# First loads of a four-layer kernel: x blocks in order on one DMA queue, first weights on the other, one warm-up matmul fewer

## The chip, the cores and the metric

The kernel runs on one core of a Trainium2 chip. The metric is the device time of one execution in microseconds (us), given as the median of several. "Before" and "after" are the kernel without and with the change. The record marks every execution as fast, and all of them are compared. Medians of a run and of the kernel before beside it are from the same chip; traces compared with each other are from several.

## The reference, cut to what matters

```python
x = A_x                                            # (1, 2048, 1024) bf16
x = x + A(layernorm(x), A_wqkv, A_wo)              # linear attention, 32 heads
x = x + B(layernorm(x), B_W_gate, B_W_up, B_W_down)   # gated MLP, F = 3584
x = x + A(layernorm(x), A_wqkv, A_wo)
x = x + B(layernorm(x), B_W_gate, B_W_up, B_W_down)
```

Almost all the time is matmuls of 128x128 by 128x512 (in the trace before, TensorE is busy for 1613.2 of 1625.4 us). The change touches only the start: the first blocks of x (128 rows each) are loaded, normalised and transposed, while the first weights (the k columns of `A_wqkv`, two blocks k0 and k1 of 1 MB) are loaded. The first useful matmul needs both.

## The kernel before

```python
def head(self):
    H = self.KT // 2                                   # 4 of the 8 k-tiles
    zero = self.ep.tile([P, NW], BF16, tag="e")
    nc.vector.memset(zero, 0.0)
    idle = self.ps3.tile([P, NW], F32, tag="b")
    for _ in range(11):                                # warm-up of TensorE, result unused
        nc.tensor.matmul(idle, lhsT=zero[:, 0:P], rhs=zero, start=True, stop=True)

    k0, k1, v0, q0, q1 = (ring.place() for _ in range(5))
    self.load_x(0, 0)                   # first half of x block 0, SyncE's queue
    self.load_x(0, 1, nc.scalar)        # second half, ScalarE's queue
    k0(0, H)                            # k0a: 512 KB of weights, SyncE
    self.load_x(1, None, nc.scalar)     # x block 1, 256 KB, ScalarE
    k0(H, 2 * H)                        # k0b
    self.load_x(2); k1(); self.load_x(3)
    # ... (cut)

def block0():                           # the order of the first work
    stat(0, 0); stat(0, 1); rstd(0)     # VectorE, VectorE, VectorE + ScalarE
    stat(1, 0)                          # VectorE needs x block 1 HERE ...
    scale(0, 0); scale(0, 1)            # ... before it scales block 0
    t0 = turn(0, 0); t1 = turn(0, 1)    # TensorE transposes block 0
    t0("ss"); stat(1, 1); rstd(1)
    # ... (cut)
    k(0, 0, between)                    # first useful matmuls: 4 with k0a, then 4 with k0b
```

In what follows x0, x1 and x2 are the first blocks of x. The program puts the first statistics of x1 before the scaling of x0. In the trace before, x1 landed at 5.53 us and its statistics started at 5.55; x0's statistics were ready at 5.87, and its scaling starts at 6.16, behind those of x1: an earlier x1 could gain about 0.3 us there (an estimate, 6.16 less 5.87).

Of the kernel before, what the change touches and what calls it, by code (L numbers as in the profile page):

```python
# [80 lines left out]
class _Net:  # L81
# [131 lines left out]
    def head(self):  # L213

        nc, tc, ring = self.nc, self.tc, self.ring
        H = self.KT // 2

        zero = self.ep.tile([P, NW], BF16, tag="e")
        nc.vector.memset(zero, 0.0)
        idle = self.ps3.tile([P, NW], F32, tag="b")  # L220
        for _ in range(11):
            nc.tensor.matmul(idle, lhsT=zero[:, 0:P], rhs=zero, start=True, stop=True)

        k0, k1, v0, q0, q1 = (ring.place() for _ in range(5))
        self.load_x(0, 0)
        self.load_x(0, 1, nc.scalar)
        k0(0, H)
        self.load_x(1, None, nc.scalar)
        k0(H, 2 * H)
        self.load_x(2)  # L230
        k1()
        self.load_x(3)

        def load():
            for t in range(4, 8):
                self.load_x(t)
            q1()
            for t in range(8, self.ST):
                self.later.at(3 + (t - 8) // 2 * 2, lambda t=t: self.load_x(t))
            self.later.at(11, v0)  # L240

        src = self.xb
        self.xnT[0, 0] = self.xnTp.tile([P, self.KT, QT * P], BF16, tag="xnT", name="xnT0_0")
        stats = [self.small.tile([P, 2, nc.vector.BN_STATS_DIM], F32, tag="stats", name=f"st{j}")
                 for j in range(QT)]
        rs, xn = {}, {}

        def stat(j, c):
            self.ln_stat(j, src[j], c, stats[j])

        def rstd(j):
            rs[j] = self.ln_rstd(stats[j])
            xn[j] = self.xn_home(0, j)

        def scale(j, h=None):
            self.ln_scale(src[j], *rs[j], xn[j], h)

        def turn(j, h):
            tp = self.ps3.tile([P, H, P], BF16, tag="b")
            for i in range(H):  # L260
                kt = h * H + i
                nc.tensor.transpose(tp[:, i, :], xn[j][:, kt * P:(kt + 1) * P], self.ident)  # L262
            dst = self.xnT[0, 0][:, h * H:(h + 1) * H, j * P:(j + 1) * P]

            def take(engine):
                if engine == "v":
                    nc.vector.tensor_copy(out=dst, in_=tp)
                elif engine == "s":
                    nc.scalar.activation(out=dst, in_=tp, func=ACT.Copy)
                else:  # L270
                    for i in range(0, H, 2):
                        nc.scalar.activation(out=dst[:, i:i + 2, :], in_=tp[:, i:i + 2, :],  # L272
                                             func=ACT.Copy)

            return take

        return load, q0, H, xn, stat, rstd, scale, turn
# [466 lines left out]
```

## Time and profile before

| | before |
|---|---|
| median (3 runs) | 1627.14 us (1626.99 to 1627.36) |
| profiled span | 1625.4 us |
| TensorE busy | 1613.2 us, 99% |
| x1 lands / first transposes / first useful matmul | 5.53 / 6.62 / 7.49 us |
| k0a, k0b, k1 land | 6.1, 7.6, 11.3 us |

The lines of the profile are in the prediction. In a chain of waits each piece is start, length, what; a DMA piece lasts from its issue to its landing. Lines of single groups give start, length, engine (SPq and ACTq are the sequencers of SyncE and ScalarE as they issue DMAs), source line and count. In lines of DMA queues q1 is SyncE's and q10 ScalarE's.

### The profile page before, as it was taken

Reading aid. Unit: us, or ns where it says so; the run is one execution under the profiler, and the core shown is the slowest. Engines: PE = TensorE matmul, PEld = TensorE weight load, DVE = VectorE, ACT = ScalarE, POOL = GpSimd, SP = SyncE. Lnnn points to the kernel's source line nnn. Section 1 sums busy time; section 2 is a strip of 40 time slices with the busy share of each in tenths; the row PEclk is TensorE's granted clock in tenths of the full one; section 3 lists DMA queues with packets and bytes.
Section 4 is the critical chain, followed back from the end, with each engine's and each line's share of the span. In section 5 each row is a group of like instructions: output and inputs, shape, how many; then the busy total and the mean of one; then the engine's idle time right before and its main releaser. Section 6 shows DMA issues by size and latency. Waiting matters only on the chain.

```text
span 1625.4 us, 18607 instructions
## 1 busy us (share of the span) xinstructions
PE 1613.2 (99%) x7605; PEld 739.4 (45%) x7739; DVE 567.7 (35%) x940; ACT 330.4 (20%) x635; POOL 202.1 (12%) x134
## 2 busy tenths in 40 slices
PE   9999999999999999999999999999999999999999
PEld 4444444444444444444444444444444444444444
DVE  8844694113212222222264447932021112111211
ACT  6741212101110210111067312121011101101110
POOL 1449220000000000000023582100000000000000
PEclk9999999999999999999999999999999999999999
DMA  9314547447455545544550157464654455454442
GB/s 269 55 52 66 172 79 203 146 158 215 156 162 195 156 147 165 160 154 139 166 111 1 54 107 240 86 189 145 193 161 152 154 178 155 146 170 150 155 162 71
DMA packets 300358, 235.58 MB, mean 145 GB/s; under 512 B 103408, under 2 KB 296304, under 8 KB 300272
## 3 DMA queue, kind: packets, MB, share of 16 engines
q1 hardware_dynamic: 294192, 228.75, 48.3%
q10 hardware_dynamic: 6080, 5.64, 1.0%
q8 instruction: 60, 0.98, 0.3%
q14 instruction: 26, 0.21, 0.0%
HBM read 201.33 MB, written 8.39 MB: 129 GB/s over the span
## 4 chain that ended last, share of the span: by engine, by line
PE 99%; issue 0%; DMA 0%; DVE 0%; ACT 0%
PE pu L643 24%; PE pg L643 24%; PE acc L667 23%; PE ps L410 14%; PE ps L536 7%; PE ps L445 7%; PE kv L458 0%; PE acc_last L667 0%; DMA x<-in_A_x_dram 0%; PE fold L521 0%; PE tp L262 0%; PE ps L435 0%; ACT L692 0%; DVE xo L684 0%; DVE x L156 0%
## 5 line engine op out<-in xcount | busy, mean ns | idle before, releaser
L643 PEld LDWEIGHTS <-t 128*128 128x128 bf16 x3584 | 350.7, 98 | 422.8
L643 PE MATMUL pu<-xnT,t 128*128 128x512 bf16 x1756 | 420.1, 379 | 2.0
L643 PE MATMUL pg<-xnT,t 128*128 128x512 bf16 x1756 | 419.8, 379 | 1.8
L667 PE MATMUL acc<-t,hT 128*128 128x512 bf16 x1728 | 380.6, 379 | 1.9
L649 DVE TENSOR_TENSOR hT<-pu,rg 128x512 bf16<-128x512 f32 x224 | 154.8, 691 | 571.5 <-PE pu L643 555.0
L648 ACT ACTIVATE rg<-pg 128x512 f32<-128x512 f32 x224 | 133.5, 596 | 736.1 <-PE pg L643 661.7
L667 PEld LDWEIGHTS <-hT 128*128 128x128 bf16 x1820 | 178.1, 98 | 209.0
L410 PE MATMUL ps<-t,xnT 128*128 128x512 bf16 x1024 | 223.4, 379 | 0.2 <-ACT xnT L272 0.2
L410 PEld LDWEIGHTS <-xnT 128*128 128x128 bf16 x1024 | 99.4, 98 | 120.0 <-issue 1.5
L536 PE MATMUL ps<-T,pqT 128*128 128x512 bf16 x500 | 110.2, 379 | 0.6
L147 ACT ACTIVATE rstd<-mv,eps 128x1 f32<-128x1 f32 x64 | 18.8, 294 | 337.7 <-DVE mv L145 337.5
L684 DVE TENSOR_TENSOR xo<-x,acc 128x512 bf16<-128x512 f32 x31 | 21.3, 687 | 170.3 <-PE acc L667 169.5
L489 POOL TENSOR_TENSOR prod<-pq,zrow 128x1024 f32<-128x1024 bf16 x32 | 68.0, 2125 | 85.9 <-DVE den L494 72.4
L140 DVE BATCH_NORM_STATS2 stats<-x 128x6 f32<-128x512 f32 (+1 forms) x120 | 77.9, 671 | 1.2 <-DMA x<-in_A_x_dram 0.4
L536 PEld LDWEIGHTS <-pqT 128*128 128x128 bf16 x512 | 49.9, 98 | 60.4 <-issue 0.5
L425 POOL CAST ksum<-x 128x512 f32<-128x512 bf16 x2 | 1.7, 866 | 605.4 <-DVE x L361 605.4
L681 DVE TENSOR_TENSOR x<-x,acc 128x512 f32<-128x512 f32 x32 | 21.6, 674 | 138.5 <-PE acc L667 137.4
L427 POOL TENSOR_TENSOR ksum<-ksum,slab 128x512 f32<-128x512 f32 x46 | 54.1, 1183 | 80.3 <-DVE slab L361 63.0
L361 DVE SCALAR_TENSOR_TENSOR pq<-ps,e 128x512 bf16<-128x512 f32 x64 | 43.9, 686 | 53.3 <-ACT e L355 51.3
L501 POOL TENSOR_TENSOR pq<-pq,den 128x1024 bf16<-128x1024 bf16 x32 | 61.7, 1936 | 3.1 <-DVE den L496 3.1
L494 DVE TENSOR_REDUCE den<-prod 128x32 f32<-128x1024 f32 x32 | 38.9, 1217 | 54.0 <-POOL prod L489 54.0
L445 PE MATMUL ps<-slab,x 128*128 128x512 bf16 x249 | 55.7, 379 | 0.4
(57 smaller groups left out, 592.5 us busy)
## 6 DMA issues: line engine op xcount, KB each, us to landing
t<-in_B_W_gate_dram SPq DMA_DIRECT2D x56, 1024.0 KB, 7.3
t<-in_B_W_up_dram SPq DMA_DIRECT2D x56, 1024.0 KB, 5.4
t<-in_B_W_down_dram SPq DMA_DIRECT2D x64, 896.0 KB, 5.1
t<-in_A_wqkv_dram SPq DMA_DIRECT2D x10, 1024.0 KB, 5.1
t<-in_A_wo_dram SPq DMA_DIRECT2D x4, 1024.0 KB, 6.7
away<-x SPq DMA_DIRECT2D x8, 512.0 KB, 4.7
x<-away SPq DMA_DIRECT2D x8, 512.0 KB, 8.2
out_dram<-xo ACTq DMA_DIRECT2D x31, 128.0 KB, 2.5
```

The lines of the kernel that those rows point to most:

```text
L140: self.nc.vector.bn_stats(out=stats[:, c, :], in_=src[:, c * fmax:(c + 1) * fmax])
L361: nc.vector.scalar_tensor_tensor(out=out, in0=ps, scalar=0.0, in1=e, op0=ALU.max, op1=ALU.add)
L410: nc.tensor.matmul(by_row(ps), lhsT=self.xnT[l, l_q][:, kt, j * P:(j + 1) * P], rhs=w[:, kt, :].rearrange("p (b i d) -> p i b d", i=R, d=H ...
L427: nc.gpsimd.tensor_tensor(out=ksum[:, cols], in0=ksum[:, cols], in1=pk, op=ALU.add)
L445: nc.tensor.matmul(ps, lhsT=self.xn[l, t][:, d * P:(d + 1) * P], rhs=self.pk[l, t][:, h * NW:(h + 1) * NW], start=(t == 0), stop=(t == sel ...
L489: nc.gpsimd.tensor_tensor(out=prod, in0=pq_of[sc, j], in1=zrow, op=ALU.mult)
L501: nc.gpsimd.tensor_tensor(out=heads(pq), in0=heads(pq), in1=den[:, :].unsqueeze(2).to_broadcast([P, D // HD, HD]), op=ALU.mult)
L536: nc.tensor.matmul(ps, lhsT=pqT[sc][:, g, j * P:(j + 1) * P], rhs=T[g // 2][:, g % 2, n2 * NW:(n2 + 1) * NW], start=(g == 0), stop=(g == G ...
L643: nc.tensor.matmul(ps, lhsT=w[:, kt, fi * P:(fi + 1) * P], rhs=self.xnT[l, q][:, kt, :], start=(kt == 0), stop=(kt == KT - 1))
L648: nc.scalar.activation(out=rg, in_=pg, func=ACT.Relu)
L649: nc.vector.tensor_tensor(out=h[:, fi, :], in0=pu, in1=rg, op=ALU.mult)
L667: nc.tensor.matmul(ps[:, 0:n], lhsT=hT[ft // 4][:, ft % 4, j * P:(j + 1) * P], rhs=wd[:, k, i * n:(i + 1) * n], start=(ft == 0), stop=(ft ...
```

## The change

It is meant to let x0 and x1 arrive first and in order, with the weights behind them, so that the first transposes come sooner. The tiny memset into the weights' tile stands behind the memset of zeros on VectorE, so ScalarE's issue of k0a has to wait for it ("the hold" in what follows). One idle matmul goes, since the useful work was to start sooner.

```diff
-        for _ in range(11):
+        for _ in range(10):
             nc.tensor.matmul(idle, lhsT=zero[:, 0:P], rhs=zero, start=True, stop=True)
 ...
         self.load_x(0, 0)
-        self.load_x(0, 1, nc.scalar)
-        k0(0, H)
-        self.load_x(1, None, nc.scalar)
-        k0(H, 2 * H)
+        self.load_x(0, 1)
+        self.load_x(1)
+
+        nc.vector.memset(ring.get((0, "k0"))[:, 0, 0:2], 0.0)
+        k0(0, H, nc.scalar)
+        k0(H, 2 * H, nc.scalar)
         self.load_x(2)
```

## The prediction

> **What bounds the kernel now.** I read the page's busy shares first, then its chain of work that ended last.
>
> ```profile
> PE 1613.2 (99%) x7605; PEld 739.4 (45%) x7739; DVE 567.7 (35%) x940; ACT 330.4 (20%) x635; POOL 202.1 (12%) x134
> ...
> PE 99%; issue 0%; DMA 0%; DVE 0%; ACT 0%
> ```
>
> TensorE is busy for 1613.2 of 1625.4 us, so every wait of it in the whole program adds up to 12.2 us. That is 0.75% of the span, and no change of the start can be worth 2%. The change touches only the first DMA issues, so I cut the chain to its first 12 us.
>
> ```profile
> 1.19 4.34 DMA x<-in_A_x_dram
> 5.53 0.02 issue
> 5.55 0.03 DVE st L140
> 5.58 0.58 issue
> 6.16 0.41 DVE x L156
> ...
> 6.62 0.41 PE tp L262 x4
> ...
> 7.49 1.47 PE ps L410 x6
> ```
>
> The columns are start, length and what. The second x block (x1, 256 KB), issued by ScalarE at 1.19 us, lands at 5.53; the first statistics of x1 then occupy VectorE until 6.16; the scaling of block 0, behind them in program order, goes until 6.57; the first transposes start at 6.62 and the first useful matmuls at 7.49. The third view is busy time of TensorE by stretch.
>
> ```profile
> 7.50:11.40 3.90, 3.90 (x24) 1.00 1.08 357
> 11.40:60.00 48.60, 48.60 (x226) 1.00 0.73 182
> ```
>
> From 7.5 us on TensorE has no gap, so a shift of this point is a shift of the end, unless another wait takes its place. The view of waits of the weight loads, from 7 to 60 us, shows a candidate.
>
> ```profile
> PEld L410 <- DMA t<-in_A_wqkv_dram: 0.2, 1, 0.2
> ```
>
> That load starts at 11.32 us, in the stretch around it, and it waits for the second block of weights, k1: issued at 2.75, 8.5 us to landing, so 11.25 to 11.3. Its matmul starts at 11.45, right behind the one before it. So k1 lands about 0.12 us before it would stop TensorE.
>
> The issues in order of time, on SyncE and then on ScalarE:
>
> ```profile
> 0.74 0.40 SPq L372 DMA_DIRECT2D x<-in_A_x_dram  x1
> 1.19 0.97 SPq L36 DMA_DIRECT2D t<-in_A_wqkv_dram  x2
> 2.20 0.50 SPq L372 DMA_DIRECT2D x<-in_A_x_dram  x1
> 2.75 0.57 SPq L36 DMA_DIRECT2D t<-in_A_wqkv_dram  x1
> ...
> 0.76 0.88 ACTq L372 DMA_DIRECT2D x<-in_A_x_dram  x2
> ```
>
> Asked one at a time, they land at: x0 first half 3.7, second half 4.0, x1 5.5, first half of the first weights (k0a, 512 KB) 6.1, second half (k0b) 7.6, x2 8.3, k1 11.3. The DMA engines are full from about 2.5 us (336 GB/s and more in each half microsecond).
>
> [...]x1 (2 KB packets) runs beside k0a (1 KB packets), from 4.0 to 4.5 us:
>
> ```profile
> q10 hardware_dynamic: 62, 0.12, 63.8%
> q1 hardware_dynamic: 69, 0.07, 39.7%
> ```
>
> 62 packets against 69, so x1 gets about two bytes for each byte of weights. But a late stretch of the same trace limits this. The output write that ScalarE issued at 1308.8, 0.7 us after SyncE had issued 1 MB of weights, moved nothing from 1309 to 1312.2: only SyncE's queue is in the list there.
>
> ```profile
> q1 hardware_dynamic: 797, 0.82, 91.9%
> issues: line engine op xcount, KB each, median us to landing
> out_dram<-xo ACTq DMA_DIRECT2D x1, 128.0 KB, 5.0
> ```
>
> It landed after 5.0 us, where such writes with no load in front took 1.7. Likewise ScalarE's q0 weights, issued at 8.09 while k1 was in flight, have no packet from 8.5 to 10.5. So between the two queues a large transfer that was issued first mostly keeps its turn. Taking turns shows only for x1 and k0a, which were issued in the same hundredth of a microsecond.
>
> [...]the idle matmuls are 0.43 us apart, the useful ones 0.216.
>
> **The change part by part.** *One idle matmul fewer* takes 0.43 us of TensorE's work: the idle ones end at about 5.6 instead of 6.0. The first transposes wait for data until 6.62, so this is worth nothing by itself.
>
> *The second half of x0 moves to SyncE.* It is issued some 0.4 us later (1.16 instead of 0.76), but without the other queue in its way. VectorE needs it only after the first half's statistics (3.78 to 4.43), and it landed at 3.96. Estimated effect on block 0: none, at best 0.2 us sooner if the first half, now alone, lands sooner.
>
> *x1 moves to SyncE*, as its third issue, at about 1.6 us instead of 1.19.
>
> *The first weights move to ScalarE*, behind a VectorE memset of two columns (about 0.06 us, like the memsets of eps), which stands behind the memset of zeros (ends at 1.28). So k0a is issued at about 1.4 us, still 0.2 us before x1. If the transfer issued first keeps its turn, x1 now waits for nearly all of k0a. What does that cost? Up to 5.0 us the queues moved 199 GB/s x 5 us = 0.995 MB, 972 KB; x0 and x1 are 512 of them, so k0a already had some 460 of its 512 KB when x1 was done. Having k0a wholly ahead costs (512 - 460) KB at about 363 KB per us, 0.14 us. The first matmul then comes at 7.6.
>
> *k0b, x2, k1.* Up to the last byte of k1 the bytes are the same as before (x0, x1, x2, k0, k1), the engines are full in both, and x3 stays behind k1. So k1 lands at about 11.3 again, give or take 0.1. k0b now runs beside x2 rather than ahead of it: between 7.6 (as now) and 8.3 (x2's landing now). Its first matmul, the fifth of its group, stands at 8.36 now, so it just fits.
>
> **Sum.** In the order of issue: +0.14 us (x1 behind k0a), k0b in time, k1 in time: 1627.3. If instead x1 follows x0 at once, x1 lands by about 5, VectorE does x1's statistics while ScalarE makes rstd, and the transposes start 0.2 to 0.4 us sooner; but then k1 stops TensorE, and only about 0.1 us is left: 1627.0.
>
> **Rivals.** (1) *k1 becomes the wait* and eats the gain: the 0.2 us wait at 11.32 speaks for it. Time 1627.0 to 1627.1. (2) *The queues share packet by packet throughout*, so that k0a and k0b get half the rate against x1, x2 and k1. Then k0a lands at about 7 and k0b at about 9.8 (its last 512 KB at some 175 KB per us), the fifth matmul slips from 8.36 to about 9.8, and the time is near 1628.6. The turns of 4.0 to 4.5 us speak for it, the late output write and q0 against it. A milder form, k1 taking turns with the last quarter of k0b, costs 0.3 us. (3) *The clock*: with one idle matmul fewer TensorE idles from 5.6 until over 6.2. [...]the first useful matmuls run at 0.43 us apart instead of 0.216, up to about 1 us lost. [...](4) *Everything hidden*: no change at all.
>
> **Range and chances.** I give the order of issue half the weight (1627.2 to 1627.5), a gain capped by k1 three tenths (1626.9 to 1627.1), full sharing and the clock a tenth each (1628 to 1628.7). The middle is 1627.25. The three runs before spread by 0.4 us, so I take 1626.7 to 1628.3. Two per cent are 32 us, more than all of TensorE's idle time, so "within" gets 0.99.
>
> **What would show it right or wrong.** The issues: x1 on SyncE near 1.6, k0a on ScalarE near 1.4. Landing of x1: 5.6 to 5.7 if k0a goes first, 5.0 or less if not. First transposes: 6.7 against 6.2 to 6.4. A wait of TensorE for weights near 8.4 would show rival 2, one near 11.3 rival 1, useful matmuls 0.43 us apart rival 3. The stretch from 12 to the end should keep its length. Wrong it would be if that stretch changed, or if the moved q0 or transposes delayed TensorE later.

Measured: 62 packets against 69, 797 against none, and matmuls 0.43 and 0.216 us apart. 1627.14 and 0.14 us make 1627.3. Rival 3's "up to about 1 us" is the author's estimate, and its working is not given.

## The result

The changed kernel takes 1629.62 us (1629.35 to 1630.89, 6 runs); the kernel before 1627.36 in 6 runs. That is 2.26 us slower, 0.14%, and outside the predicted range. The ratio given is 1.0015, 95% interval 1.0003 to 1.0028. Ratios here are the mean time of one kernel's fast runs over that of the other's of the same rounds, so not quite the ratio of the medians.

Busy time and chain on the page of the changed kernel:

```profile
PE 1621.3 (100%) x7738; PEld 739.9 (45%) x7738; DVE 567.7 (35%) x941; ACT 330.2 (20%) x635; POOL 202.1 (12%) x134
...
PE 99%; DMA 0%; issue 0%; DVE 0%; SPq 0%; ACT 0%
```

TensorE's busy time is 8 us up, but the trace before had 7605 matmul records and this one has 7738 with one matmul fewer in the program: records were missing before, and this sum says nothing. The start of the chain says more:

```profile
1.66 4.91 DMA x<-in_A_x_dram
...
6.59 0.04 DVE st L140
...
7.20 0.41 DVE x L156
...
7.65 0.62 PE tp L264 x4
...
8.73 2.42 PE ps L412 x6
```

Read it against the same pieces of before. x1 now lands at 6.56 instead of 5.53, so the scaling and the transposes are 1.03 us later. Then the pieces of TensorE themselves are longer: four transposes take 0.62 instead of 0.41, and six matmuls 2.42 instead of 1.47. In the trace the first five of them start about 0.43 us apart, as the idle matmuls do; before they were 0.22. This distance is called half clock in what follows: in e1 and e5, after their rest, the granted-clock column reads 0.50 while useful matmuls are 0.43 us apart. Together 1.03 + 0.21 + 0.95 = 2.19 us, and the spans differ by 2.1. After that nothing moves: TensorE has no gap in the stretch that had none before.

```profile
11.40:60.00 48.60, 48.60 (x229) 1.00 0.76 186
```

The issues (SyncE, then ScalarE) are where the prediction put them: x1 is SyncE's third, at 1.66, and k0a is issued at 1.34.

```profile
0.74 1.82 SPq L374 DMA_DIRECT2D x<-in_A_x_dram  x4
2.60 0.43 SPq L36 DMA_DIRECT2D t<-in_A_wqkv_dram  x1
...
1.34 0.99 ACTq L36 DMA_DIRECT2D t<-in_A_wqkv_dram  x2
```

Busy time by stretch shows what the queues moved (the last number is GB/s), first before, then after:

```profile
0.00:5.00 5.00, 3.66 (x9) 1.34 (x10) 1.68 (x6) 1.28 (x1) 0.70 (x6) 1.00 0.57 199
2.50:4.00 1.50, 1.50 (x5) 0.57 (x4) 0.22 (x1) 0.00 (x0) 0.00 (x0) 1.00 1.04 367
```
```profile
0.00:5.00 5.00, 3.66 (x9) 1.34 (x10) 1.73 (x7) 1.28 (x1) 0.70 (x6) 1.00 0.58 151
2.50:4.00 1.50, 1.50 (x5) 0.58 (x4) 0.69 (x1) 0.00 (x0) 0.00 (x0) 1.00 0.84 143
```

Before, the engines were full from 2.5 us (share 1.04, 367 GB/s up to 4 us); after, there is a hole from 2.5 to 4 us (0.84, 143 GB/s). It does not need k0a in front: the traces of e4, e7 and e10 below, where k0a is issued after x1, have it too (262, 216 and 264 GB/s in that stretch), and so do e1, e2 and e11 (197, 276, 270), while the seven traces in which weights are issued by 0.8 us or x0 and x1 come over both queues have 342 to 367. And from 4 to 5 us x1 (q1) gets few turns:

```profile
q10 hardware_dynamic: 247, 0.25, 71.5%
q1 hardware_dynamic: 73, 0.13, 34.5%
```

That is 73 packets against 247, where before, from 4.0 to 4.5 us, x1 had 62 against 69.

The granted-clock column reads 1.00 in the first microseconds of both traces, although the idle matmuls there are 0.43 us apart: it has no record yet. The clock records in the packed traces begin with full clock at 5.68 us before and at 10.70 after, in line with the distances. So in the changed kernel's trace TensorE did not lose the full clock in its rest: all ten idle matmuls are at half clock, and it had not come to full clock when the useful work began. The column shows the half clock only in traces where the clock was full first and fell back (e1, e5, e6, e10).

### The profile page after: what moved, and what is told of

Read it like the earlier page. It is cut to its first block, busy times and chain, and to the rows that moved or that the text cites. A ratio compares the mean times of both kernels' runs of the same rounds, so it can differ in the third digit from the quotient of the medians.

```text
span 1627.5 us, 18740 instructions
## 1 busy us (share of the span) xinstructions
PE 1621.3 (100%) x7738; PEld 739.9 (45%) x7738; DVE 567.7 (35%) x941; ACT 330.2 (20%) x635; POOL 202.1 (12%) x134
## 4 chain that ended last, share of the span: by engine, by line
PE 99%; DMA 0%; issue 0%; DVE 0%; SPq 0%; ACT 0%
PE pu L645 24%; PE pg L645 24%; PE acc L669 23%; PE ps L412 14%; PE ps L538 7%; PE ps L447 7%; PE kv L460 0%; PE acc_last L669 0%; DMA x<-in_A_x_dram 0%; PE fold L523 0%; PE tp L264 0%; PE ps L437 0%; SPq L374 0%; DVE xo L686 0%; DVE x L156 0%
```

## The experiments

Theory A has two parts. (1) x1 waits because k0a, issued before it on the other queue, keeps its turn. (2) TensorE, with nothing to do from about 5.8 to 7.65 us, is at half clock when the useful work comes. Each part should be worth about half of the loss. The rivals are named in each run's expectation.

All runs in one table. The traced execution's times are in us from the start of the span; "step" is the distance of the first useful matmuls; "median" is of all runs, with the median of the kernel before on the same chip. The label e9 was given to no run.

| run | k0a issued | x1 issued, landed | transposes | matmuls from, step | median | before there |
|---|---|---|---|---|---|---|
| before | 1.19 | 1.19, 5.53 | 6.62 | 7.49, 0.22 | 1627.14 | |
| after | 1.34 | 1.66, 6.56 | 7.65 | 8.73, 0.43 | 1629.62 | 1627.36 |
| e1: 11 idle | 1.34 | 1.66, 7.18 | 8.28 | 9.31, 0.43 | 1629.81 | 1627.60 |
| e2: 15 idle | 1.34 | 1.66, 6.16 | 7.33 | 8.19, 0.22 | 1628.64 | 1627.60 |
| e3: before, 10 idle | 1.20 | 1.19, 5.16 | 6.25 | 7.13, 0.22 | 1627.15 | 1627.60 |
| e4: k0 on SyncE | 2.13 | 1.66, 4.40 | 5.49 | 6.36, 0.22 | 1628.20 | 1627.60 |
| e5: no hold | 0.76 | 1.66, 7.24 | 8.32 | 9.20, 0.43 | 1630.44 | 1627.15 |
| e6: hold on k0a only | 3.95 | 1.66, 5.90 | 6.98 | 12.79, 0.43 | 1634.25 | 1627.15 |
| e7: e4, k1 before x2 | 2.13 | 1.66, 5.80 | 6.89 | 7.97, 0.43 | 1628.98 | 1627.15 |
| e8: before, 4 idle | 1.20 | 1.19, 5.31 | 6.40 | 7.48, 0.43 | 1628.94 | 1627.15 |
| e10: long hold | 2.13 | 1.66, 4.67 | 5.76 | 7.16, 0.22 | 1631.79 | 1627.04 |
| e11: after again | 1.34 | 1.66, 6.46 | 7.55 | 8.64, 0.43 | 1629.99 | 1627.04 |
| e12: x1 alone on ScalarE | 1.66 | 0.76, 3.97 | 6.34 | 7.49, 0.22 | 1628.47 | 1627.04 |
| e13: same, x2 before k1 | 1.66 | 0.76, 4.01 | 6.39 | 7.47, 0.22 | 1628.39 | 1627.04 |

The intervals of the ratios are about 0.14% to either side, some 2.3 us, so the times alone settle little: only the change itself, e5, e6, e10 and e11 have an interval that leaves out 1. The traces carry most of the argument, and each run has only one. All runs gave correct results.

### e1_after_idle11: the changed kernel with eleven idle matmuls

```diff
-        for _ in range(10):
+        for _ in range(11):
```

> The changed kernel with eleven idle matmuls again. The changed kernel lost about 1.03 us because x1 lands at 6.56 instead of 5.53, and about 1.16 us because its first transposes and five matmuls run at half clock (release at about 10.7 us). Theory A (the clock is lost to TensorE's 2.07 us without work before the first transposes, mostly because x1 is late): one more idle matmul shortens the gap only to 1.65 us, so at most a few tenths come back: 1629.2 to 1629.7. Rival B (the removed idle matmul alone lost the clock): 1628.4 to 1628.6, first useful matmuls 0.216 us apart.

Measured: 1629.81 us (1630.14, 1630.35, 1629.49 and one of 1627.80, which has no trace and stays unexplained). One idle matmul does not bring the time back, so rival B falls, as does any reading by which the first line of the diff is the cost. In this trace the clock has records. Columns: stretch, length, busy time and count of TensorE, then the granted clock:

```profile
5.00:8.30 3.30, 0.68 (x4) 1.00 1.06 367
8.40:11.70 3.30, 3.25 (x14) 0.50 1.08 345
11.80:15.00 3.20, 3.20 (x22) 1.00 0.91 303
```

TensorE was at full clock when its idle matmuls ended at 5.66 (1.00 in the column), rested until 8.28 because x1 landed at 7.18, and was then at half clock (0.50 from 8.4 to 11.7 us), just when the useful work came: 14 starts in 3.3 us, where 22 fit in 3.2 (1.00 again from 11.8). So in this trace a rest of 2.6 us was followed by half clock. In e5 it is much the same: a rest of 2.5 us, transposes at full clock from 8.32 (four in 0.41 us), then half clock from 9.5 to 12.8 (0.50 in the column).

### e2_after_idle15: the changed kernel with fifteen idle matmuls

```diff
-        for _ in range(10):
+        for _ in range(15):
```

> The changed kernel with fifteen idle matmuls, which at half clock reach to 7.74 us, about where the transposes start (7.65). Theory A: TensorE is released before the useful work, which then runs at 0.216 us a matmul; x1 stays late at about 6.6. Loss of about 1.1 us left: 1628.3 to 1628.6. Rival C (the half clock of the useful matmuls comes from something else, or costs nothing at the end): 1629.4 or more.

Measured: 1628.64 us on the same chip (1627.83 to 1629.07), 1.17 us less than with eleven.

```profile
1.34 6.15 PE idle L222 x15
...
8.19 1.47 PE ps L412 x6
```

The idle matmuls reach to the transposes, and six useful matmuls take 1.47 us again, as before the change. What remains, 1.04 us over the kernel before in the medians, goes with the late x1 (6.16): in the traces the useful matmuls start 0.70 us later than before (8.19 against 7.49), and the spans differ by 0.6. That 1.17 and 1.04 add up to about the whole loss is no evidence, as their sum is e1's loss by construction; and x1 landed 1.0 us later in e1's trace than in this one, so their difference is not the clock alone. From 3 to 4 us the queues show why x1 is late:

```profile
q10 hardware_dynamic: 260, 0.27, 87.1%
q1 hardware_dynamic: 6, 0.01, 2.4%
```

x1 was issued at 1.66, and from 3 to 4 us SyncE's queue, with the last of x0 and then x1, hardly moves: 260 of the 266 packets are ScalarE's, which k0a heads.

### e3_before_idle10: the first line of the change alone

```diff
-        for _ in range(11):
+        for _ in range(10):
```

> The kernel before with ten idle matmuls: the change's first line alone. Theory A: its gap before the transposes grows from 0.6 to 1.04 us; x1 lands at 5.5 as before; the clock is released in time: 1627.1 to 1627.5. Rival B (the removed idle matmul alone loses the clock): about 1628.3 to 1628.5, useful matmuls 0.43 us apart at first.

Measured: 1627.15 against 1627.60, the same; useful matmuls 0.22 us apart. In this trace x1 landed at 5.16 already, so TensorE rested for only 0.5 us, not the 1.04 of the expectation; for the longer rest there are only the four times (1626.95 to 1627.71), none of which shows a loss. Ten idle matmuls were enough here. The trace also has TensorE wait 0.5 us for k1, which landed at 11.77.

### e4_weights_sync: k0 behind the x blocks on SyncE

```diff
-        k0(0, H, nc.scalar)
-        k0(H, 2 * H, nc.scalar)
+        k0(0, H)
+        k0(H, 2 * H)
```

> The changed kernel with the first weights on SyncE's queue, behind x0 and x1; all else stays, ten idle matmuls included. Theory A (x1 is late because ScalarE's k0 goes in between): x1 lands by 5.0, transposes start at 6.2 to 6.4, the clock is released in time or nearly, and k1 at about 11.3 caps the gain: 1626.9 to 1627.4. Rival D (x1 as third issue on SyncE is late by itself, because three issues stand one behind the other): x1 lands after 5.5 and the time stays over 1628.

Measured: 1628.20 us. x1, with the same place on the same queue, lands at 4.40 and the transposes start at 5.49, two microseconds sooner than in the changed kernel. That speaks for theory A and against rival D's third issue, though e7 below puts x1 at 5.80 with the same first five issues, so the gain differs much between executions. The time is no better than before: it misses theory A's 1626.9 to 1627.4 and is what rival D had named (over 1628), for another reason. Waits of TensorE, 0 to 20 us:

```profile
PE ps L412 <- DMA t<-in_A_wqkv_dram: 2.9, 2, 1.7
```

With seven issues one behind the other on SyncE (0.40 to 0.51 us each), k1 is issued at 3.70 instead of 2.75 and lands at 13.49; k0b lands at 9.01. In this execution the 16 engines also finished far apart (by the trace's landings, k0b's shares from 7.16 to 9.01, k1's from 11.10 to 13.49), and the matmuls behind k1 started at 13.54, after the last share. An x1 that landed 2.16 us sooner than in the changed kernel was worth nothing here, as the weights came later for it.

### e5_no_hold: the changed kernel without the memset

```diff
-        nc.vector.memset(ring.get((0, "k0"))[:, 0, 0:2], 0.0)
```

> The changed kernel without the memset that holds the weights: ScalarE issues k0a at about 0.76 us, beside the first half of x0, and k0b at 1.2. Theory A (a large transfer that was issued first keeps its turn until little of it is left): the second half of x0 (issued at 1.19) and x1 (1.66) both start late, so VectorE's second statistics start after 5.0 instead of 4.43, x1 lands at 7 to 8, the transposes start at 8 or later, the first useful matmuls run at half clock: 1630 to 1632. Rival E (the queues share packet by packet): x1 lands at about 5.5 to 6.5, no later than with the hold; 1628 to 1629.7.

Measured: 1630.44 us. k0a, issued at 0.76, lands at 4.53; the second half of x0 (issued at 1.19) only at 5.16, and x1 at 7.24. All as theory A expected, and rival E (packet-by-packet sharing, which cannot hold back 128 KB until 512 KB are through) falls for the x blocks. The hold of the change does serve its purpose for x0 (its second statistics start at 4.43 with it, at 5.19 here); it is too short for x1 (6.56 with it).

### e6_long_hold: a longer hold, done wrong

```diff
-        nc.vector.memset(ring.get((0, "k0"))[:, 0, 0:2], 0.0)
+        for _ in range(3):
+            nc.vector.memset(ring.get((0, "k0"))[:, 0, :], 0.0)
```

> The changed kernel with a hold of about 0.8 us more (three memsets of 128x512 in place of the one of two columns), so that ScalarE issues k0a at about 2.1 us, after SyncE's x1 (1.66). Theory A (order of issue decides): x1 lands at 4.3 to 4.8, transposes start at 5.5 to 6.0 right after the idle matmuls, no half clock for useful matmuls; the landings of k0b and k1 then hold TensorE, so the time is about that of the kernel before, within 0.8 us. Rival E (sharing with the other queue delays x1 whenever ScalarE's weights run beside it): x1 lands after 5.5, transposes after 6.6, time over 1628.5.

Measured: 1634.25 us. This misses its aim. The memsets cover only the first half of the tile, so the second half, k0b, was free to go and was issued at 0.76, beside the first half of x0. The third memset slipped behind the first statistics, so k0a was issued at 3.95, after k1 (2.60) and x3 (3.07). It landed at 12.75:

```profile
PE ps L413 <- DMA t<-in_A_wqkv_dram: 5.1, 1, 5.1
```

As an experiment on holds it fails. Against rival E it still speaks: 512 KB issued last of the first eight came in last of them, 8.8 us after their issue.

### e10_hold_both: the long hold, done right

```diff
-        nc.vector.memset(ring.get((0, "k0"))[:, 0, 0:2], 0.0)
+        nc.vector.memset(ring.get((0, "k0"))[:, :, 0:192], 0.0)
```

> The long hold done right (in the run before, the hold covered only the first half of the weights, and the second half was issued at 0.76 us, ahead of everything): one memset of about 0.8 us over both halves, so ScalarE issues k0a at about 2.1 us and k0b at 2.6, behind SyncE's x1 (1.66), beside x2 and k1. Theory A (order of issue decides): x1 lands at 4.3 to 5.8, so before the 6.16 to 7.18 seen with the short hold; k0a lands after 6, k0b after 8.5 because x2 and k1 stand beside it, and TensorE then waits for k0b; 1627.5 to 1630. Rival E (k0 on the other queue delays x1 even when it is issued later): x1 lands at 6.2 or later.

Measured: x1 lands at 4.67, the transposes start at 5.76. Only the moment at which ScalarE's weights are issued (k0a and, behind it, k0b) differs from the changed kernel (k0a at 2.13, after x1's 1.66, instead of 1.34, before it), and x1 comes 1.9 us sooner. This is the cleanest test of part (1): queues and order on each queue are the same. The time is another matter, 1631.79 us, outside the expectation. k0b was issued at 2.61 on ScalarE's queue, k1 at 2.60 on SyncE's, and from 7.5 to 10 us the two move nearly the same number of packets:

```profile
q1 hardware_dynamic: 431, 0.44, 54.5%
q10 hardware_dynamic: 427, 0.43, 54.1%
```

k0b, needed at about 8, lands at 10.97, and TensorE waits for weights 3.2 us, 2.8 of them at one place. After that rest TensorE is at half clock too: 0.50 in the column from 11.0 to 13.8 us, an estimated 1.4 us more (half of 2.8). The two transfers, issued within 0.01 us of each other, shared evenly (431 packets against 427), as x1 and k0a did in the kernel before (62 against 69).

### e8_before_idle4: half clock alone

```diff
-        for _ in range(11):
+        for _ in range(4):
```

> The kernel before with four idle matmuls instead of eleven: its loads and landings stay, TensorE rests from about 3.05 us to the transposes at 6.2 to 6.6. Theory A (TensorE without work for two or three microseconds ahead of the useful work runs it at half clock at first): first useful matmuls 0.43 us apart[...], loss of 1.5 to 3.5 us: 1629 to 1631. Rival C (half clock at the start costs nothing at the end, because k0b and k1 are waited for anyway): within 0.5 us of the kernel before.

Measured: 1628.94 against 1627.15, 1.8 us more, with the loads of the kernel before untouched:

```profile
1.19 4.12 DMA x<-in_A_x_dram
...
7.48 2.57 PE ps L410 x6
```

x1 lands even sooner (5.31), the useful matmuls start where they did (7.48), but six of them take 2.57 us instead of 1.47, and four transposes 0.62 instead of 0.41: 1.31 us in this trace. The median is a little under the expected 1629 to 1631, which was the author's estimate. So here the half clock alone costs over a microsecond, as part (2) says, and rival C falls.

### e11_after_again: the changed kernel a second time

> The changed kernel once more, unedited, for a second trace of it on this chip and a second set of times. Theory A: the weights issued at 1.34 go before x1 again, x1 lands at 6.1 to 7.2, the queues move markedly less up to 5 us than the 0.995 MB of the kernel before, useful matmuls start at half clock in most executions: 1.5 to 3 us over the kernel before. Rival G (the late x1 of the first trace was an accident of one execution): x1 lands before 5.8.

Measured: 1629.99 us on another chip, 2.95 over the kernel before there; x1 at 6.46, so rival G falls. The matmuls stay at half clock longer than in the first trace (the first six take 2.74 us against 2.42). From 4 to 5 us:

```profile
q10 hardware_dynamic: 253, 0.26, 72.7%
q1 hardware_dynamic: 74, 0.13, 35.2%
```

Up to 5 us the queues moved 186 GB/s here, not 151, and x1 was late all the same. So the hole in the transfers is not the constant part; the uneven turns are.

### e7_k1_first, e12_x1_scalar, e13_x1_scalar_x2_first: tries at a better order

```diff
 e7, from e4:                 e12, from before:                    e13: as e12, but
-        self.load_x(2)       -  self.load_x(0, 1, nc.scalar)
         k1()                 +  self.load_x(1, None, nc.scalar)
+        self.load_x(2)       +  self.load_x(0, 1)
         self.load_x(3)          k0(0, H)
                              -  self.load_x(1, None, nc.scalar)
                                 k0(H, 2 * H)
                              -  self.load_x(2)                        +  self.load_x(2)
                                 k1()                                     k1()
                              +  self.load_x(2)                        -  self.load_x(2)
                                 self.load_x(3)                           self.load_x(3)
```

> All first loads on SyncE in the order x0, x0, x1, k0a, k0b, and then k1 ahead of x2 (which is needed later); ten idle matmuls. Weights behind x1 on one queue let x1 land at 4.4 and the transposes start at 5.49, but matmuls waited for k0b (2.04 us before the fourth-to-fifth step) and k1. Theory A (with x1 early, the landings of k0b and k1 are the next limit): k1 lands about 0.7 us sooner, and the time falls by some 0.3 to 0.9 us against the same order with x2 ahead; against the kernel before of the same runs between -0.8 and +0.4 us. Rival F (x2 now late stalls VectorE and so TensorE later): slower than the kernel before by 0.5 us or more.

> A try at a better order from the kernel before (eleven idle matmuls): x1 is ScalarE's first and only issue (0.76 us), SyncE issues both halves of x0, then k0a (1.66), k0b, k1, and x2 after k1. Theory A: x0 and x1 land by 4.5, transposes start right after the idle matmuls at 6.0 to 6.1, in time for the full clock, first useful matmuls at 6.9 to 7.0 or when k0a lands (about 6); k1 lands at 10.5 to 11.3: 0.2 to 0.8 us faster than the kernel before. Rival F (k0, k1 or the late x2 becomes the wait): same or slower.

> The same with x2 ahead of k1, as in both kernels. Theory A: transposes early as in the run before it, but k1 lands at 11.3 to 12 and holds TensorE, so the gain over the kernel before is gone: -0.3 to +0.5 us against it. Rival F (x2 after k1 costs more than it brings): faster than the run with k1 ahead.

Measured: 1628.98, 1628.47 and 1628.39 us against 1627.15, 1627.04 and 1627.04. None beats the kernel before, and all three expectations of theory A miss (that of e13 allowed 0.5 us over the kernel before and got 1.35). Rival F (slower) fits the times of e7 and e12, but in e7 not for its reason: TensorE does not wait for weights there. In e7's trace x1 lands at 5.80, the transposes come at 6.89, and the useful matmuls are 0.43 us apart after a rest of only 1.1 us (here too the clock had not been full: its records begin at 10.80).

```profile
1.66 4.14 DMA x<-in_A_x_dram
```
```profile
2.50:4.00 1.50, 1.50 (x5) 0.57 (x4) 0.93 (x2) 0.00 (x0) 0.00 (x0) 1.00 0.85 216
```

This limits part (1). Nothing stood on ScalarE's queue, and x1 was still 1.4 us later than in e4, after the same hole in the transfers. Over all traces, with k0a issued before x1 (the changed kernel, e1, e2, e5, e11) x1 lands from 6.16 to 7.24; with k0b alone before it (e6) at 5.90; behind x0 alone (e4, e7, e10) from 4.40 to 5.80. The order of issue separates the groups, but how much it is worth differs between executions by a microsecond or more. Why is not shown.

In e12 and e13 x1 lands at about 4.0 and the useful matmuls are at full clock from the start (in e13 the transposes, 0.11 us apart, are not yet), but x0 does not gain by it (its second half lands at 4.3), and with k0a issued at 1.66 instead of 1.19 the weights are late. Waits of TensorE in e13:

```profile
PE ps L410 <- DMA t<-in_A_wqkv_dram: 1.3, 2, 0.8
```

The order of k1 and x2 made no difference that these runs can tell (1628.47, 1628.39).

## Why the prediction was wrong

**Right: the bound and the order.** Nothing after 12 us moved, the loss stayed far below 2%, and the issues stood where they were put. The bound was read from a trace in which 134 matmul records are missing (7605 of 7739), so the 12.2 us of waits are too many (the changed kernel's trace leaves 6.2), and it bounds a gain only: e6 lost 7 us. The chosen mechanism, "the transfer issued first keeps its turn" so that x1 waits for k0a, is what e5, e10 and e4 show in kind (x1 at 7.24 with k0a issued before it, at 4.67 and 4.40 with k0a after it), with e7 (5.80) as a limit to its size. Of the first line, "worth nothing by itself" agrees with e3 and e1 within the noise.

**Wrong, first step: the size of x1's delay.** The prediction wrote "Having k0a wholly ahead costs (512 - 460) KB at about 363 KB per us, 0.14 us". It measured 1.03 us in the first trace. The sum counts bytes and leaves the rate as it was ("the engines are full in both", as the prediction says of k1). Both terms were too small. The rate: 151 GB/s up to 5 us instead of 199, or 0.24 MB less, at 0.372 MB per us (372 GB/s from 2.5 to 6 us in the trace before) 0.65 us. The bytes: at 6.0 us SyncE's queue had just moved x0 and x1, and ScalarE's had moved 0.61 MB, all of k0a and some of k0b, where before 0.47 MB of k0a had gone when x1 was through at 5.0 (SyncE's 0.60 MB less half of x0). These 0.14 MB are 0.38 us. Both are estimates from queue totals; together they are the 1.03. In e11 (186 GB/s; 0.62 MB at 5.74) the same working gives 0.17 and 0.40 us, and x1 still landed at 6.46, so how the delay divides differs between executions. Why x1's turns are so few beside a transfer issued 0.3 us before it, and what makes the hole, is not shown by any run.

**Wrong, second step: the clock as a side bet.** Rival 3 had a tenth of the weight and "up to about 1 us", argued from the idle matmul removed; what was said against it rested on a figure that no trace here shows. The half clock came true in both traces of the changed kernel (matmuls 0.43 us apart), at about the size named; the reason given, one idle matmul fewer, did not: with it put back (e1) the useful work is at half clock all the same, and without it alone (e3) at full. The missing thought was that the clock is not independent of the first step: the late x1 lengthened the rest of TensorE from 0.6 to 1.9 us. In the traces the first useful matmuls were at full clock after rests of up to 0.8 us (e12) and at half clock after 1.1 us (e7) and more; in e7 and the changed kernel the clock had not been full before. Where the line lies is not shown. The half clock cost 0.21 + 0.95 = 1.16 us in the trace, and alone in e8 1.31 in the trace, 1.8 in the medians. When full clock comes differs between executions (5.68 and 6.32 us in the traces of before and e3, 10.70 and 13.69 in those of the changed kernel), so part of it may be chance. In the five traces with k0a ahead of x1, useful work ran at half clock in all but e2, whose idle matmuls fill the rest.

**Right by luck: the weights.** k0b was to land "between 7.6 (as now) and 8.3", and k1 "at about 11.3 again". They landed at 9.62 and 11.74. TensorE did not wait only because the late and slow start had moved k0b's first matmul to 10.41. Had it stood at 8.5 (8.36 and the 0.14 of the forecast), it would have waited some 1.1 us (an estimate from this trace's landing). So a cure of x1 and the clock alone would not have given the whole loss back in this execution.

**Rival 1** (k1 caps a gain) was not put to the test by the change, there being no gain. **Rival 2** (sharing throughout) falls by e5 for the x blocks. For k0b beside x2 and k1 its landing "at about 9.8" came true (9.62), and from 6.5 to 8.5 us the two queues did share, 337 packets on SyncE's and 303 on ScalarE's. The wait that it forecast was hidden in the changed kernel; in e4, e6, e10, e12 and e13 weights did hold TensorE.

## What to carry to other kernels

In these runs x1 landed sooner where it was issued before k0a (3.97 to 5.80 us in e4, e7, e10, e12 and e13) than where it was issued after it (6.16 to 7.24), so what is urgent should be issued first in time. A hold for the less urgent transfer has to outlast the issue of the urgent one: k0a went at 1.34 and x1 at 1.66, so the hold was over 0.3 us too short (e10's was 0.8 us longer), and each issue in front cost the next transfer 0.4 to 0.5 us (0.40 to 0.51 in e4). Warm-up matmuls should last until the useful work really starts: with eleven that ended 2.6 us before it the first six useful matmuls took 2.67 us (e1), with fifteen that reached to it 1.47 (e2). So when a change can delay that start, their number is to be re-sized with it and not ahead of it. Check in the trace the distance of the first matmuls, not the clock column alone. And none of the tried orders beat the kernel before. What no run tried is to take x1's first statistics out of the way of x0: in the changed kernel's trace x0's statistics were ready at 5.93 us and its scaling started at 7.20, behind x1.
